# A fused attention and expert kernel: gate logits of three units worked on in their PSUM bank, and the last listed tile behind all dense tiles

## The chip, the cores and the metric

The kernel runs on one core of a Trainium2 chip. The metric is the time of one execution on the device, in microseconds; lower is better. A core has TensorE (PE: matmuls; PEld its weight loads), VectorE (DVE), ScalarE (ACT), GpSimd (POOL) and SyncE (SP, which here only starts transfers). Each works through its own queue in order; semaphores tie them together.

## What is computed

Four batches of 11,456 rows of 128 numbers go through two steps of attention by way of 49 agents, and each resulting row then through one of eight experts, the one with the largest gate logit:

```python
def _attn_ref(q, k, v, agents):
    def sm(a, b):
        s = scale * (a @ b.transpose(0, 2, 1))
        s = s - s.max(-1, keepdims=True)
        e = np.exp(s)
        return e / (e.sum(-1, keepdims=True) + 1e-09)
    return sm(q, agents) @ (sm(agents, k) @ v)

# x: the 45,824 rows of the attention; F = 1024
logits = x @ w_gate                                  # 8 experts
expert_idx = np.argmax(logits, axis=1)
probs = softmax(logits)                              # + 1e-09 in the sum
y[row] = probs[row, e] * (np.maximum(x[row] @ w1[e], 0) @ w2[e])   # e = expert_idx[row]
```

## The kernel before

**Tiles and stages.** A batch is 90 blocks of 128 rows. Ten blocks are a *unit* (`UB`), nine units a batch. For each batch come: the agents' scores against the keys (`k_ops`), the agents' sums over the values (`v_ops`), the queries' scores and exponentials (`q_head`, one unit at a time, stored to memory and read back transposed as `et`), the gates, the routing (`r_ops`: which expert each row has, and lists), and the experts.

**Dense and listed tiles.** In each batch most rows have the same expert. Every row is first put through it: `dense_tile` takes 4, 4 and 2 blocks of a unit (`MACROS`), stores the result and so fills the whole output. The rows whose expert is another are listed; a *listed* tile (`min_tile`) of 128 of them is gathered, put through its expert, and scattered over the dense result by POOL (L1430). `CAP` allows 8, 5, 1 and 1 listed tiles for the four batches. A loop over the batches (`seq`, `ready`) sets the order of dense and listed tiles: the tiles of batches 0 to 2 are mixed into the next batch's dense tiles, that of batch 3 goes in after `(3, 8, 0)`, the first 4 blocks of its last unit.

**An expert tile.** Layer one goes into an `hp` bank pair (L1194 and, for the small terms, L1203; L1187 to L1189 in a listed tile). ACT makes the rounded half `hhi` (L1223), DVE the remainder `hlo` (L1228), which frees `hp`. Layer two adds both in `yp` (L1211, L1212, L1217), of which there is one buffer; ACT copies it to `yo` (L1328), POOL multiplies by the gate `isc` (L1333), SP stores (L1338, L1341).

**The gates.** `q_tail` does a unit: ten matmuls (L925) give, for each row, eight high parts of the logits, eight low parts and a sum, 17 numbers in the PSUM bank `misc`; ACT copies the high parts to `lg` in SBUF (L930), DVE adds the low parts (L933) and puts the sum into `sm` (L934). Then the bank is free. `gate_ops` does two units (`GP = 2`) from SBUF: the largest logit (L950), the reciprocal (L951), the difference (L952), the product (L953), the exponential on ACT (L956), and the gate `isc` (L960 to L964), all on DVE.

**One bank for many.** PSUM has one `misc` buffer. Scores (L372 to L374), agent sums (L514), gates, routing counts (L1141) and the turned rows of listed tiles (L1405) all pass through it, one at a time.

**The order of the work.** The functions only record operations, with a cost, a key (when it is due) and the buffers they take and use. `Plan.run` then lays them out for all engines at once: of the operations that are ready and no more than `WINDOW = 20` keys ahead, it takes the one that can start first by those costs, and an operation that takes a buffer waits until the last user of the old one is done (`RINGS` says how many buffers there are). So a change of one cost or one buffer can change the order everywhere.

Of the kernel before, what the change touches and what calls it, by code (L numbers as in the profile page):

```python
# [56 lines left out]
GP = 2  # L57
# [147 lines left out]
def agent_attention_moe(ctx: ExitStack, tc: tile.TileContext, qT, kT, v, agT, wg, w1, w2, out):  # L205
# [620 lines left out]
    def q_begin(t, key):  # L826
        t.glg, t.gsm, t.gisc = Gen("lg"), Gen("sm"), Gen("isc")

        def begin():
            t.lg = buf("lg", [P, NBLK, NE])  # L830
            t.sm = buf("sm", [P, NBLK])
# [5 lines left out]
        t.o_qb = PL.op("POOL", 1.0, begin, key, new=[t.glg, t.gsm, t.gisc])  # L837
# [79 lines left out]
    def q_tail(t, u, k):  # L917
        U = t.U[u]
        r = Rec()
        gp = Gen("misc")  # L920

        def lo():
            p = r.l = misc([P, UB, LW])
            for j in range(UB):
                nc.tensor.matmul(p[:, j], U.et.bitcast(F16)[0:A2, j * P:(j + 1) * P], t.G, start=True, stop=True)  # L925

        sl = slice(u * UB, (u + 1) * UB)

        def lc():
            nc.scalar.copy(t.lg[:, sl], r.l[:, :, 0:NE])  # L930

        def la():
            nc.vector.tensor_tensor(t.lg[:, sl], r.l[:, :, NE:2 * NE], t.lg[:, sl], op=OP.add)  # L933
            nc.vector.tensor_scalar(t.sm[:, sl], r.l[:, :, 2 * NE], 1e-9, None, op0=OP.add)  # L934
        U.o_lo = o = PL.op("PE", 0.26, lo, k, U.o_et + [t.o_G, t.o_qb], new=[gp], use=[U.gt, t.gG])
        o = PL.op("ACT", act(UB * NE), lc, k, [o, t.o_qb], use=[gp, t.glg])
        U.o_lg = PL.op("DVE", 0.36, la, k, [o], use=[gp, t.glg, t.gsm])


    def gate_ops(t, u0, u1, k):  # L940
# [3 lines left out]
        g3, g4 = Gen("gz"), Gen("gr")  # L944

        def g1():
            z = r.z = buf("gz", [P, GP * UB, NE])[:, 0:n]
            rs = r.rs = buf("gr", [P, 3, GP * UB])[:, :, 0:n]
            lg = t.lg[:, sl]
            nc.vector.tensor_reduce(rs[:, 2], lg, axis=AX.X, op=OP.max)  # L950
            nc.vector.reciprocal(rs[:, 0], t.sm[:, sl])  # L951
# [3 lines left out]
        def g2():  # L955
            nc.scalar.activation(r.z, r.z, AF.Exp, scale=1.0 / SW)  # L956
# [13 lines left out]
        for U in t.U[u0:u1]:  # L970
            U.o_gate = o
# [699 lines left out]
```

## Time and profile before

| | |
|---|---|
| three runs | 1016.14, 1010.60, 1016.64 us; median 1016.14 |
| the profiled execution | 1012.58 us, its span 1010.7 us |
| PE busy | 940.8 us, 93% of the span |
| DVE, ACT, POOL busy | 733.0, 661.6, 515.1 us |
| granted PE clock, mean | 0.98 |

The profile is of one execution. Busy time of PE counts matmuls whose ends are modelled, so where PE is busy it need not run at its best. A row of the time line gives start, duration, engine, line, operation, output and input, count, and in brackets the idle time of that engine just before with what ended it. In a row by line, busy time and the mean in ns of one stand behind the first bar, the idle time before it and its releasers behind the second. A row of waits gives the total, the number of times and the longest. Where an engine waits for several, the last to come is named.

### The profile page before, as it was taken

How to read it: one execution, taken by the hardware profiler on the slowest of the kernel's cores; microseconds unless marked ns; L12 is line 12 of the kernel's file. 1: busy time of each engine (PE TensorE's matmuls, PEld its weight loads, DVE VectorE, ACT ScalarE, POOL GpSimd, SP SyncE). 2: the span in 40 equal slices, each digit the busy share in tenths (PEclk: the TensorE clock that was granted, in tenths of full speed). 3: DMA queues.
4: the chain of work that ended last, by engine and by line, in shares of the span. 5: the costliest groups of instructions: out<-in, count | busy, mean ns of one | idle time of the engine just before them, and what ended most of it. 6: DMA issues, size and time to landing. Idle time of an engine off the chain costs nothing. (4 is left out here: it accounts for less than half of the span.)

```text
span 1010.7 us, 34717 instructions
## 1 busy us (share of the span) xinstructions
PE 940.8 (93%) x14953; PEld 766.1 (76%) x14953; DVE 733.0 (73%) x1148; ACT 661.6 (65%) x898; POOL 515.1 (51%) x721
## 2 busy tenths in 40 slices
PE   5789998999899999999998998999999999999895
PEld 4668876877678877878777887888877788777674
DVE  7656677588996677566899767676788966778852
ACT  6457986877686777644576777764666667656453
POOL 4124988555495988332345488742234535321321
PEclk9999998999999999999999999999999999999998
DMA  9636788885579566565444926881444635331211
GB/s 339 203 116 228 237 276 226 249 256 197 177 236 251 168 196 192 146 184 174 112 134 128 311 76 185 208 233 39 133 115 108 175 91 143 77 93 45 71 28 31
DMA packets 157261, 166.41 MB, mean 165 GB/s; under 512 B 60618, under 2 KB 130503, under 8 KB 157098
## 3 DMA queue, kind: packets, MB, share of 16 engines
q1 hardware_dynamic: 155658, 163.17, 54.0%
q8 instruction: 119, 1.95, 0.8%
q0 software_dynamic: 1440, 0.93, 0.5%
q14 instruction: 44, 0.36, 0.1%
HBM read 99.73 MB, written 45.57 MB: 144 GB/s over the span
## 5 line engine op out<-in xcount | busy, mean ns | idle before, releaser
L1228 DVE SCALAR_TENSOR_TENSOR hlo<-hp,hhi 128x1024 f16<-128x1024 f32 x375 | 445.9, 1218 | 180.9 <-ACT hhi L1223 178.5
L1223 ACT ACTIVATE hhi<-hp 128x1024 f16<-128x1024 f32 x375 | 368.9, 1023 | 161.5 <-PE hp L1203 142.8
L1211 PE MATMUL yp<-Wd,hhi 128*128 128x128 f16 x2880 | 354.3, 222 | 1.2 <-ACT yo L1328 0.7
L1212 PE MATMUL yp<-Wd,hhi 128*128 128x128 f16 x2880 | 352.9, 222 | 0.0
L1211 PEld LDWEIGHTS <-hhi 128*128 128x128 f16 x3000 | 293.7, 99 | 32.8 <-issue 29.7
L1212 PEld LDWEIGHTS <-hhi 128*128 128x128 f16 x3000 | 298.0, 99 | 2.5 <-issue 2.1
L1333 POOL TENSOR_TENSOR yo<-yo,isc 128x256 f32<-128x256 f32 x180 | 112.6, 643 | 235.6 <-ACT yo L1328 183.9
L1194 PE MATMUL hp<-et,Md 128*128 128x512 f16 (+1 forms) x864 | 195.0, 346 | 22.9 <-DVE hlo L1228 22.7
L352 POOL TENSOR_TENSOR clo<-cf,chi 128x512 f16<-128x512 f32 x186 | 185.1, 1026 | 54.2 <-ACT chi L344 43.9
L1217 PE MATMUL yp<-Wd,hlo 128*128 128x128 f16 x2880 | 192.9, 219 | 0.5 <-DVE hlo L1228 0.5
L1217 PEld LDWEIGHTS <-hlo 128*128 128x128 f16 x3000 | 176.2, 98 | 2.8 <-issue 1.5
L1194 PEld LDWEIGHTS <-Md 128*128 128x128 f16 x864 | 75.0, 98 | 63.7 <-issue 30.2
L1328 ACT COPY yo<-yp 128x512 f32<-128x512 f32 (+1 forms) x108 | 55.7, 516 | 71.1 <-PE yp L1217 54.3
L876 POOL TENSOR_TENSOR rows<-xs,rows 128x245 f16<-128x245 f32 x72 | 46.8, 670 | 99.6 <-ACT rows L871 93.7
L344 ACT CAST chi<-cf 128x1280 f16<-128x1280 f32 x62 | 78.3, 1264 | 6.9 <-DMA cf<-in_qT 4.6
L1203 PE MATMUL hp<-etq,Mq 19*128 19x512 f16 (+1 forms) x864 | 72.1, 352 | 0.0
L1203 PEld LDWEIGHTS <-Mq 19*128 19x128 f16 x864 | 18.8, 91 | 69.6 <-issue 69.6
L374 PEld LDWEIGHTS <-clo 128*128 128x128 f16 x670 | 54.2, 97 | 3.3 <-POOL clo L352 3.0
L372 PE MATMUL misc<-a,chi 128*128 128x49 f16 x630 | 55.7, 184 | 0.6 <-DVE xt L1426 0.5
L374 PE MATMUL misc<-a,clo 128*128 128x49 f16 x630 | 55.5, 184 | 0.7 <-POOL clo L352 0.7
L373 PE MATMUL misc<-a,chi 128*128 128x49 f16 x630 | 55.4, 185 | 0.0
L372 PEld LDWEIGHTS <-chi 128*128 128x128 f16 x630 | 50.4, 96 | 5.0 <-issue 3.2
(263 smaller groups left out, 1167.2 us busy)
## 6 DMA issues: line engine op xcount, KB each, us to landing
cf<-in_kT SPq DMA_DIRECT2D x36, 640.0 KB
cf<-in_v SPq DMA_DIRECT2D x35, 640.0 KB
cf<-in_qT SPq DMA_DIRECT2D x35, 640.0 KB
out<-yo SPq DMA_DIRECT2D x72, 256.0 KB
eb<-rows SPq DMA_DIRECT2D x36, 320.0 KB
wf<-in_w SPq DMA_DIRECT2D x16, 512.0 KB
vst<-parts SPq DMA_DIRECT2D x15, 512.0 KB
wst<-parts SPq DMA_DIRECT2D x15, 512.0 KB
```

The costliest lines, as they stand in the source:

```text
L344: nc.scalar.copy(st.hi[:, i * n:(i + 1) * n], f)
L352: (nc.gpsimd if pool else nc.vector).tensor_tensor(st.lo[:, o], f[:, d], st.hi[:, o], op=OP.subtract)
L372: nc.tensor.matmul(p[:, j], h, t.a[:, 0], start=True, stop=False)
L374: nc.tensor.matmul(p[:, j], l, t.a[:, 0], start=False, stop=True)
L1194: nc.tensor.matmul(hp[:, c:c + n], m[:, fb * P:(fb + 1) * P], e, start=c % 512 == 0, stop=False)
L1203: nc.tensor.matmul(hp[:, c:c + n], m[r:r + R2, fb * P:(fb + 1) * P], e[r:r + R2], start=False, stop=(c + n) % 512 == 0)
L1211: nc.tensor.matmul(y, h, w[:, fb * 256 + P:(fb + 1) * 256], start=first and j == 0 and i == 0, stop=False)
L1212: nc.tensor.matmul(y, h, w[:, fb * 256:fb * 256 + P], start=False, stop=False)
L1217: nc.tensor.matmul(yp[:, j * P:(j + 1) * P], lo[:, c + j * P:c + (j + 1) * P], w[:, fb * 256:fb * 256 + P], start=False, stop=last and j = ...
L1223: nc.scalar.activation(hi, hp, AF.Relu)
L1228: nc.vector.scalar_tensor_tensor(lo, hp, 0.0, hi, op0=OP.max, op1=OP.subtract)
L1333: nc.gpsimd.tensor_tensor(v3[:, j:j + 2], v3[:, j:j + 2], t.isc[:, k0 + j:k0 + j + 2, 1:2].bitcast(F32).to_broadcast([P, 2, P]), op=OP.mult)
```

## The change

`q_tail` goes. `gate_ops` does what it did and more, for the units in `GROUPS`: unit 0, units 1 and 2, units 3 to 5, units 6 to 8. Up to 30 blocks' logits (510 numbers a row) lie in one `misc` bank. ACT copies the high parts to a new tile `lm`; DVE adds them to the low parts in the bank, adds 1e-9 to the sums in the bank, and takes reciprocal, largest logit, difference and product from there; only the product is written to SBUF, in `lg`. The bank is free after that sixth instruction. The exponential reads `lg` and writes `gz`. The last step, `isc`, moves from DVE (one instruction) to POOL (two). Routing reads `lg`, which now holds the product in place of the difference; it tests for zero in both cases.

Batch 3's listed tile is called for at `(3, 8, 8)`, the last blocks of its last unit, and is no longer held back by `gap`. The scatter (L1428 in the changed kernel) depends on all stores recorded before it, so now on all of batch 3's. Three smaller edits: `an` and `idx` have one buffer, and a listed tile takes its `xt` buffer with the matmul before it and not with ACT's copy.

```diff
-GP = 2
+GP = 3
-RINGS = {... "an": 2, ... "lg": 2, "sm": 2, "idx": 2, ...}
+RINGS = {... "an": 1, ... "lg": 2, "idx": 1, ...}
...
-    def q_tail(t, u, k):
...
     def gate_ops(t, u0, u1, k):
...
+        def lo():
+            p = r.l = misc([P, GP * UB, LW])[:, 0:n]
+            for i, U in enumerate(us):
+                for j in range(UB):
+                    nc.tensor.matmul(p[:, i * UB + j], U.et.bitcast(F16)[0:A2, j * P:(j + 1) * P], t.G, start=True, stop=True)
+
+        def lc():
+            r.m = buf("lm", [P, GP * UB, NE])[:, 0:n]
+            nc.scalar.copy(r.m, r.l[:, :, 0:NE])
 
         def g1():
...
-            lg = t.lg[:, sl]
-            nc.vector.tensor_reduce(rs[:, 2], lg, axis=AX.X, op=OP.max)
-            nc.vector.reciprocal(rs[:, 0], t.sm[:, sl])
-            nc.vector.tensor_tensor(lg, lg, rs[:, 2, :, None].to_broadcast([P, n, NE]), op=OP.subtract)
-            nc.vector.tensor_tensor(z, lg, rs[:, 0, :, None].to_broadcast([P, n, NE]), op=OP.mult)
+            l = r.l[:, :, NE:2 * NE]
+            nc.vector.tensor_tensor(l, l, r.m, op=OP.add)
+            nc.vector.tensor_scalar(r.l[:, :, 2 * NE], r.l[:, :, 2 * NE], 1e-9, None, op0=OP.add)
+            nc.vector.reciprocal(rs[:, 0], r.l[:, :, 2 * NE])
+            nc.vector.tensor_reduce(rs[:, 2], l, axis=AX.X, op=OP.max)
+            nc.vector.tensor_tensor(l, l, rs[:, 2, :, None].to_broadcast([P, n, NE]), op=OP.subtract)
+            nc.vector.tensor_tensor(t.lg[:, sl], l, rs[:, 0, :, None].to_broadcast([P, n, NE]), op=OP.mult)
...
+        def g5():
+            rs = r.rs
             sv = t.isc[:, sl, 1:2].rearrange("p k o -> p (k o)").bitcast(F32)
-            nc.vector.scalar_tensor_tensor(sv, rs[:, 0], t.isig, rs[:, 1], op0=OP.mult, op1=OP.mult)
+            nc.gpsimd.tensor_tensor(rs[:, 0], rs[:, 0], rs[:, 1], op=OP.mult)
+            nc.gpsimd.tensor_scalar(sv, rs[:, 0], t.isig, None, op0=OP.mult)
...
-            o = PL.op("PE", 0.12, mm, k + 1, [o, t.o_av2], new=[gx], use=[gec, t.gav2])
-            o = PL.op("ACT", act(P), hi, k + 1, [o], new=[x.gxt], use=[gx])
+            o = PL.op("PE", 0.12, mm, k + 1, [o, t.o_av2], new=[gx, x.gxt], use=[gec, t.gav2])
+            o = PL.op("ACT", act(P), hi, k + 1, [o], use=[gx, x.gxt])
...
-    ready = {(1, 2, 0): 0, (2, 2, 0): 1, (3, 2, 0): 2, (3, 8, 0): 3}
+    ready = {(1, 2, 0): 0, (2, 2, 0): 1, (3, 2, 0): 2, (3, 8, 8): 3}
...
-                if wait and gap >= 6:
+                if wait and (gap >= 6 or c == B - 1):
...
+    GROUPS = ((0, 1), (1, 3), (3, 6), (6, 9))
...
-                q_tail(t, u, k + 6)
-            if u % GP == 1 or u == NU - 1:
-                gate_ops(t, u - u % GP, u + 1, k + 8)
+            for u0, u1 in GROUPS:
+                if u == u1 - 1 and (t.b or u > 2):
+                    gate_ops(t, u0, u1, k + 7)
```

What the planner makes of it shows in the queues. First DVE at the start of the program, where the gates of batch 0's unit 0 meet the first expert tiles; before:

```order
L1228 SCALAR_TENSOR_TENSOR hlo<-hp,hhi 128x1024
L933 TENSOR_TENSOR lg<-misc,lg 128x80
L934 TENSOR_SCALAR sm<-misc 128x10
L1228 SCALAR_TENSOR_TENSOR hlo<-hp,hhi 128x1024
L859 TENSOR_REDUCE qm<-misc 128x10
L863 TENSOR_TENSOR xs<-misc,qm 128x490
```

and now (line numbers are those of the changed kernel; `lm` is the copy of the high parts, `gr` holds maxima and reciprocals):

```order
L1226 SCALAR_TENSOR_TENSOR hlo<-hp,hhi 128x1024
L937 TENSOR_TENSOR misc<-misc,lm 128x10x8
L938 TENSOR_SCALAR misc<-misc 128x10
L939 RECIPROCAL gr<-misc 128x10
L940 TENSOR_REDUCE gr<-misc 128x10
L941 TENSOR_TENSOR misc<-misc,gr 128x10x8
L942 TENSOR_TENSOR lg<-misc,gr 128x80
L1226 SCALAR_TENSOR_TENSOR hlo<-hp,hhi 128x1024
```

Six instructions on the bank stand between the two `hlo` where two stood. Second, DVE in batch 1, the gates of units 4 and 5 before, and of units 3 to 5 now (`vacc` are the agent sums of batch 2, which use the same bank); before:

```order
L1228 SCALAR_TENSOR_TENSOR hlo<-hp,hhi 128x1024
L933 TENSOR_TENSOR lg<-misc,lg 128x80
L934 TENSOR_SCALAR sm<-misc 128x10
L950 TENSOR_REDUCE gr<-lg 128x20
L951 RECIPROCAL gr<-sm 128x20
L952 TENSOR_TENSOR lg<-lg,gr 128x160
L953 TENSOR_TENSOR gz<-lg,gr 128x160
L960 TENSOR_REDUCE gr<-gz 128x20
L961 TENSOR_SCALAR gr<-gr 128x20
L962 RECIPROCAL gr<-gr 128x20
L964 SCALAR_TENSOR_TENSOR isc<-gr,isig 128x20
L524 TENSOR_TENSOR vacc<-vacc,misc 49x129 x2
```

and now:

```order
L1226 SCALAR_TENSOR_TENSOR hlo<-hp,hhi 128x1024
L937 TENSOR_TENSOR misc<-misc,lm 128x30x8
L938 TENSOR_SCALAR misc<-misc 128x30
L939 RECIPROCAL gr<-misc 128x30
L940 TENSOR_REDUCE gr<-misc 128x30
L941 TENSOR_TENSOR misc<-misc,gr 128x30x8
L942 TENSOR_TENSOR lg<-misc,gr 128x240
L949 TENSOR_REDUCE gr<-gz 128x30
L950 TENSOR_SCALAR gr<-gr 128x30
L951 RECIPROCAL gr<-gr 128x30
L1226 SCALAR_TENSOR_TENSOR hlo<-hp,hhi 128x1024
L524 TENSOR_TENSOR vacc<-vacc,misc 49x129 x2
```

The bank is free after the second of the gate's rows before, after the sixth now; on PE's queue the agent sums' matmuls follow the 30 gate matmuls behind 16 matmuls of layer two and 8 of layer one. Third, POOL at the end of the program (`yo` multiplies, then the scatter of batch 3's listed tile); before:

```order
L1333 TENSOR_TENSOR yo<-yo,isc 128x256 x3
L1429 MEMSET spacer 1x1
L1430 DMA out<-yo,rt 45824x128
L1333 TENSOR_TENSOR yo<-yo,isc 128x256 x3
L1603 TENSOR_LOAD ovf
```

and now:

```order
L1331 TENSOR_TENSOR yo<-yo,isc 128x256 x6
L1427 MEMSET spacer 1x1
L1428 DMA out<-yo,rt 45824x128
L1601 TENSOR_LOAD ovf
```

The scatter stands behind the last dense multiply, and with it behind the last store, where three multiplies followed it.

More of the change, by code (lines that the diff above doesn't have):

```diff
@@ L61 @@
 BS = NU * US
-RINGS = {"misc": 1, "hp": 3, "yp": 1, "cf": 7, "chi": 2, "clo": 2, "xs": 2, "wf": 2, "vst": 2, "wst": 2, "an": 2, "av2": 4, "et": 5, "etq": 3,
+RINGS = {"misc": 1, "hp": 3, "yp": 1, "cf": 7, "chi": 2, "clo": 2, "xs": 2, "wf": 2, "vst": 2, "wst": 2, "an": 1, "av2": 4, "et": 5, "etq": 3,
          "rows": 2, "rt": 2, "ls": 2, "ix": 2, "er": 2, "ec": 2, "xt": 3, "hhi": 4, "hlo": 4, "yo": 4, "a16": 2, "af": 2, "qm": 2, "mh": 2,
-         "isc": 2, "G": 2, "lg": 2, "sm": 2, "idx": 2, "isig": 2, "bm": 2, "Md": 2, "Mq": 2, "Ml": 2, "Wd": 2, "ohx": 1, "oa": 2}
+         "isc": 2, "G": 2, "lg": 2, "idx": 1, "isig": 2, "bm": 2, "Md": 2, "Mq": 2, "Ml": 2, "Wd": 2, "ohx": 1, "oa": 2}
 class Op:
@@ L826, in q_begin @@
     def q_begin(t, key):
-        t.glg, t.gsm, t.gisc = Gen("lg"), Gen("sm"), Gen("isc")
+        t.glg, t.gisc = Gen("lg"), Gen("isc")
         def begin():
             t.lg = buf("lg", [P, NBLK, NE])
-            t.sm = buf("sm", [P, NBLK])
             t.isc = buf("isc", [P, NBLK, 4], I32)
@@ L836, in begin @@
             nc.gpsimd.memset(t.isc[:, :, 3:], 0)
-        t.o_qb = PL.op("POOL", 1.0, begin, key, new=[t.glg, t.gsm, t.gisc])
+        t.o_qb = PL.op("POOL", 1.0, begin, key, new=[t.glg, t.gisc])
         t.o_lg, t.o_gate, t.o_eb = [], [], []
@@ L914, in q_head @@
         U.o_et = [PL.op("ACT", act(UC), cp, k, [o], new=[gt], use=[gh])]
-    def q_tail(t, u, k):
[L918 to L937, printed above, removed]
     def gate_ops(t, u0, u1, k):
@@ L962, in g3_ @@
             nc.vector.reciprocal(rs[:, 1], rs[:, 1])
+        def g5():
+            rs = r.rs
             sv = t.isc[:, sl, 1:2].rearrange("p k o -> p (k o)").bitcast(F32)
-            nc.vector.scalar_tensor_tensor(sv, rs[:, 0], t.isig, rs[:, 1], op0=OP.mult, op1=OP.mult)
+            nc.gpsimd.tensor_tensor(rs[:, 0], rs[:, 0], rs[:, 1], op=OP.mult)
+            nc.gpsimd.tensor_scalar(sv, rs[:, 0], t.isig, None, op0=OP.mult)
         c = n * NE * 0.00107
-        o = PL.op("DVE", 0.7 + 3 * c, g1, k, [U.o_lg for U in t.U[u0:u1]], new=[g3, g4], use=[t.glg, t.gsm])
+        o = PL.op("PE", 0.04 + 0.3 * (u1 - u0), lo, k, [o for U in us for o in U.o_et] + [t.o_G, t.o_qb], new=[gp], use=[U.gt for U in us] + [t.gG])
+        for U in us:
+            U.o_lo = o
+        o = PL.op("ACT", act(n * NE), lc, k, [o, t.o_qb], new=[gm], use=[gp])
+        o = PL.op("DVE", 0.62 + 4 * c, g1, k, [o], new=[g3, g4], use=[gm, gp, t.glg])
         t.o_lg.append(o)
-        o = PL.op("ACT", act(n * NE), g2, k, [o], use=[g3])
-        o = PL.op("DVE", 0.85 + c, g3_, k, [o, t.o_sig], use=[g3, g4, t.gsig, t.gisc])
-        for U in t.U[u0:u1]:
+        o = PL.op("ACT", act(n * NE), g2, k, [o], use=[g3, t.glg])
+        o = PL.op("DVE", 0.4 + c, g3_, k, [o], use=[g3, g4])
+        o = PL.op("POOL", 0.35, g5, k, [o, t.o_sig], use=[g4, t.gsig, t.gisc])
+        for U in us:
             U.o_gate = o
@@ L1550, in agent_attention_moe @@
     t0.U[1].ld[0].after.append(t0.o_vl[-1])
-    q_tail(t0, 1, -934)
     q_head(t0, 2, -936, True)
```

11 lines of the change are left out of this document (6 added, 5 removed).

## The prediction

> **What bounds the kernel now.** I read the page first, for the busy shares of the engines.
>
> ```profile
> span 1010.7 us, 34717 instructions
> PE 940.8 (93%) x14953; PEld 766.1 (76%) x14953; DVE 733.0 (73%) x1148; ACT 661.6 (65%) x898; POOL 515.1 (51%) x721
> ```
>
> TensorE (PE) is busy for 940.8 of 1010.7 us, and the change leaves its matmuls as they are. So the change can only move the 70 us in which PE stands. Next come the waits of PE, and a table of stretches, which says where they are.
>
> ```profile
> PE hp L1194 <- DVE hlo L1228: 22.7, 22, 3.6
> PE misc L514 <- DVE xs L863: 5.1, 2, 4.2
> 0.00:25.00 25.00, 12.93 (x270) 11.72 (x270) 18.34 (x43) 16.48 (x19) 11.41 (x24) 1.00 0.93 341
> 250.00:300.00 50.00, 45.99 (x691) 35.52 (x689) 47.30 (x68) 37.56 (x46) 33.27 (x36) 0.97 0.66 215
> 700.00:750.00 50.00, 50.00 (x725) 39.32 (x722) 37.90 (x75) 29.21 (x42) 10.95 (x17) 1.00 0.38 109
> 1000.00:1011.00 11.00, 0.32 (x6) 0.14 (x3) 0.00 (x0) 0.37 (x1) 0.62 (x1) 0.68 0.12 32
> ```
>
> In a row of stretches the busy times follow as PE, PEld, DVE, ACT, POOL. The first 25 us (12 lost) and the last 11 (10.7 lost) are the load and the drain. In between PE loses 4 us in 250 to 300, where VectorE (DVE) is busy for 47.3 of 50, and nothing in 700 to 750. The stalls are local: mostly layer one of the experts (L1194) waiting for DVE's `hlo`, which frees the `hp` bank, and some waits for the one `misc` bank.
>
> The largest single wait of the middle is at 172 us, and the time line of DVE, POOL, ACT and PE around it shows what makes it.
>
> ```profile
> 164.20 5.07 DVE L952 TENSOR_TENSOR lg<-lg,gr 128x160 f32<-128x160 f32 x1
> 165.34 3.75 POOL L501 TENSOR_TENSOR S<-S,m 128x245 f32<-128x245 f32 x6
> 169.66 0.34 ACT L956 ACTIVATE gz<-gz 128x160 f32<-128x160 f32 x1 [4.25 <-DVE gz L953]
> 172.06 1.32 PE L514 MATMUL misc<-cf,S 128*49 128x129 f32 x10 [4.16 <-DVE xs L863]
> ```
>
> L952, the gates' subtraction, both of whose operands are in SBUF, stood from 164.20 to 169.27, until POOL's row of tensor operations ended at 169.1. ACT's exponential stood behind it for 4.25 us and PE for 4.16. The spread of each line says whether this is the rule.
>
> ```profile
> L952 DVE TENSOR_TENSOR lg<-lg,gr x20: 236/261/5070, 83.2 to 918.2; 128x160 f32<-128x160 f32 x16, 128x80 f32<-128x80 f32 x4
> L953 DVE TENSOR_TENSOR gz<-lg,gr x20: 241/326/3002, 83.5 to 918.4; 128x160 f32<-128x160 f32 x16, 128x80 f32<-128x80 f32 x4
> L933 DVE TENSOR_TENSOR lg<-misc,lg x36: 219/231/242, 63.8 to 917.6; 128x80 f32<-128x80 f32 x36
> ```
>
> The columns are least, median and longest ns. L933, of the same kind but with one operand in PSUM, never took over 242 ns in 36 times; L952 and L953 went up to 5070 and 3002. In this trace, only the two with both operands in SBUF stand behind POOL.
>
> The Trainium skill's page SBUF — State Buffer, section SBUF: two separate sides, says that a DVE instruction with two SBUF inputs and a GpSimd instruction that reads SBUF take turns on one port pair, each for its whole instruction. By it alone a wait would end with the POOL instruction under way; the 5.07 us outlasted a whole row of them, so the trace has more at stake than the page, and I go by the trace.
>
> **The change part by part.** *The locked pair goes.* L941 and L942 of the changed kernel do the same arithmetic with one operand in PSUM, as L933 does. Besides the 5.07 us, the long cases of L952 and L953 (3.00 at most) stand ahead of PE's waits at 370 to 372, 619 and 801 us:
>
> ```profile
> 370.00 0.28 PE L1217 MATMUL yp<-Wd,hlo 128*128 128x128 f16 x2 [0.49 <-DVE hlo L1228]
> 372.47 0.23 PE L1405 MATMUL misc<-ident,er 128*98 128x128 f16 x1 [0.51 <-DVE xs L863]
> 618.96 0.18 PE L372 MATMUL misc<-a,chi 128*128 128x49 f16 x1 [0.54 <-DVE xt L1426]
> 801.64 0.39 PE L1194 MATMUL hp<-et,Md 128*128 128x512 f16 x1 [1.48 <-DVE hlo L1228]
> 613.94 0.23 PE L1405 MATMUL misc<-ident,er 128*98 128x128 f16 x1 [2.34 <-ACT yo L1328]
> ```
>
> 4.16 + 0.49 + 0.51 + 0.54 + 1.48 = 7.2 us gained. Bounds: 4.2 (the first alone) and 7.2.
>
> *A wait with no cover.* The last row quoted is a transpose into `misc` right behind ten gate matmuls that had just filled it. In the new order no gate group is followed at once by another user of `misc`; the wait of 2.3 us goes.
>
> *Fewer instructions on DVE.* The rows by line, with their sums (three rows of ACT end the list):
>
> ```profile
> L952 DVE TENSOR_TENSOR lg<-lg,gr 128x160 f32<-128x160 f32 (+1 forms) x20 | 14.2, 712 | 0.0
> L953 DVE TENSOR_TENSOR gz<-lg,gr 128x160 f32<-128x160 f32 (+1 forms) x20 | 12.3, 615 | 0.7
> L933 DVE TENSOR_TENSOR lg<-misc,lg 128x80 f32<-128x80 f32 x36 | 8.3, 232 | 3.7 <-ACT lg L930 3.7
> L934 DVE TENSOR_SCALAR sm<-misc 128x10 f32<-128x10 f32 x36 | 5.7, 157 | 0.0
> L950 DVE TENSOR_REDUCE gr<-lg 128x20 f32<-128x160 f32 (+1 forms) x20 | 6.0, 302 | 0.0
> L951 DVE RECIPROCAL gr<-sm 128x20 f32<-128x20 f32 (+1 forms) x20 | 5.1, 256 | 0.0
> L863 DVE TENSOR_TENSOR xs<-misc,qm 128x490 f32<-128x490 f32 x36 | 24.1, 668 | 2.8
> L930 ACT COPY lg<-misc 128x80 f32<-128x80 f32 x36 | 8.1, 226 | 6.9 <-PE misc L925 6.6
> L433 ACT COPY S<-misc 128x490 f32<-128x490 f32 x27 | 15.3, 568 | 4.7 <-PE misc L374 4.4
> L1223 ACT ACTIVATE hhi<-hp 128x1024 f16<-128x1024 f32 x375 | 368.9, 1023 | 161.5 <-PE hp L1203 142.8 <-PE hp L1189 16.9 <-ACT big L1031 0.8
> ```
>
> The first six rows sum to 51.6 us. In their place come 16 groups of six. Between L933 (80 elements, 232 ns) and L863 (490, 668) lies 1.06 ns an element, so a tensor operation on 240 takes 0.40 us. A group of three units costs three of these, a reduction of 0.40 (L950 with the same step), a scalar operation of 0.18 (L934) and a reciprocal of 0.28 (L951): 2.06; a group of one about 1.3, of two 1.7. Four batches: 4 x (1.3 + 1.7 + 2 x 2.06) = 28 us. So DVE sheds 23 us, 15 of them the stalls of L952 and L953 over their medians. Beyond the waits already counted this is worth something only where DVE is full (the row 250 to 300). Gate work stands there for a few us at most, so I take 1 us gained, between nothing and 6.
>
> An operation of DVE that writes PSUM has no row here. From below, it costs what one that reads PSUM does; L934, which reads it, is the shortest of the six rows with 157 ns. From above, twice L934's time, 0.16 us on three of the six in 16 groups: 7.5 us of DVE time, under the 23 shed. I take the lower.
>
> The Trainium skill speaks against this part: its page Perfetto Trace Analysis, section Optimizing Scalar/DVE Operations, puts DVE's fixed cost near 125 ns on PSUM and 60 on SBUF. Worked out from the page, an estimate, five operations moved to PSUM in 16 groups would add 5 us to DVE; the sum would be 1 us worse at most. L934's 157 ns leave little room for such a surcharge.
>
> *The start.* In DVE's queue, six instructions of unit 0's gates now stand ahead of an `hlo` where L933 and L934 stood; the rest of its gate work came only later.
>
> ```profile
> 63.82 0.23 DVE L933 TENSOR_TENSOR lg<-misc,lg 128x80 f32<-128x80 f32 x1
> 64.04 1.22 DVE L1228 SCALAR_TENSOR_TENSOR hlo<-hp,hhi 128x1024 f16<-128x1024 f32 x1
> 64.81 0.20 PE L372 MATMUL misc<-a,chi 128*128 128x49 f16 x1
> ```
>
> DVE starts the `hlo` some 0.9 us later, and the scores at 64.81 find the bank free 0.2 us later than they ask. I take 0.5 lost, from 0 to 1.3.
>
> *The bank is held longer.* With one `misc` bank, the next user on PE's queue waits for the arithmetic's end. A group of three holds it for ACT's copy (226 ns for 80 elements and 568 for 490 give 0.36 for 240) and 2.06 on DVE: some 2.5 us. If an activation of 1.02 us (L1223) and an `hlo` of 1.22 stand ahead on the two queues, 4.8. What covers it is the layer work that PE has queued between, at these rates:
>
> ```profile
> 991.71 1.06 PE L1217 MATMUL yp<-Wd,hlo 128*128 128x128 f16 x16
> 985.34 1.03 PE L1194 MATMUL hp<-et,Md 128*128 128x512 f16 x4
> 986.30 0.40 PE L1203 MATMUL hp<-etq,Mq 19*128 19x512 f16 x4
> ```
>
> In the new order the eight groups of three have between 2.3 us (16, 4 and 4 of just these, batch 1, units 3 to 5) and over 19 ahead of the next user; four have under 3.7: 2.3, 3.2, 3.5 and 3.6. Without queueing they lose 0.2 in all; with both queues ahead 2.5 + 1.6 + 1.3 + 1.2 = 6.6. I take half, 3.3 lost. ACT has 24 instructions fewer, at 65% busy I cost that at nothing.
>
> *The end.* Batch 3's listed tile now ends the program. The tile's 24 matmuls of layer one fill what was PE's wait for the last `yo` copy; its 24 of layer two come after the last dense tile.
>
> ```profile
> 990.59 1.05 POOL L1430 DMA_INDIRECT out<-yo,rt  x1 [3.12 <-DMA out<-yo]
> 1000.40 0.37 ACT L1328 COPY yo<-yp 128x256 f32<-128x256 f32 x1 [2.97 <-PE yp L1217]
> 1000.85 0.62 POOL L1333 TENSOR_TENSOR yo<-yo,isc 128x256 f32<-128x256 f32 x1 [2.13 <-ACT yo L1328]
> 1001.88 0.92 SPq L1341 DMA_DIRECT2D out<-yo  x1
> ```
>
> Its 48 matmuls are some 3 us at 1.06 for 16, so the last dense tile ends about 2.5 us earlier. But the scatter waits for the last dense store to land (3.1 us, as at 990.59) and takes 1.05 where the program ended with the store: 0 net, from 1 gained to 3 lost.
>
> *POOL.* The product with `isig` becomes 32 short instructions there, each of 30 elements at most, so under the 0.62 us of a 256-element `yo` multiply (just above). They stand ahead of the `yo` multiplies, which waited for the gate before too. POOL is 49% idle and four `yo` buffers cover it: nothing, at most 2 us.
>
> *Waits of the new order.* It is drawn up anew everywhere, and POOL still stands against DVE's two-operand instructions in the routing. A quarter of the 7.2 comes back elsewhere: 1.7 lost, from 0 to 5.
>
> Sum: -7.2 - 2.3 - 1 + 3.3 + 0.5 + 0 + 1.7 = -5.0 us. The profiled execution took 1012.58, so 1007.6. The three runs' median is 1016.14, and those three with the profiled one average 1014.0, from which the sum gives 1009.0. I put the time at 1008.5.
>
> **The rivals.** *A: DVE's relief reaches the full stretches.* The 23 us shed shorten the queue ahead of `hlo` wherever routing and gates meet. For it: 22.7 us of PE's waits are for `hlo`. Against: the routing's own instructions fill those stretches and stay. With 6 us gained there, and 0 to 5 lost to bank and new order: 1012.58 - 7.2 - 2.3 - 6 + 0.5 = 997.6, up to 1003.
>
> *B, slower: the bank becomes the bound.* Three units' logits sit in the one `misc` bank, and PE's queue, which is in order, stops at its next user: scores, agent sums or routing counts. All eight groups of three would lose 2.5 to 3.5 us (20 to 28), less 9.5 gained: 1023 to 1031. It decides from where hold exceeds cover, 3.6 us for half the groups. For it: the 2.34 us at 613.94 is this wait. Against: one such wait in 36 groups before.
>
> *C: nothing comes of it.* PE is 93% busy, and the waits struck out return one place further on, as with 700 to 750, where PE is full whatever DVE does: 1012 to 1014.
>
> **How the numbers follow.** The forecast has 0.49, A 0.24, B 0.15, C 0.12. About 1% is what a measurement here can tell from no change. Faster by more: A and the forecast's lower edge, 0.24 + 0.09 = 0.33. Slower by more: most of B, 0.13. The rest, 0.54, is within. The range takes in the forecast with its bounds, C, and all of A but its edge, and leaves out most of B: 998 to 1021.
>
> **What would show it.** Right: no tensor operation of the gates above 0.5 us; PE's waits behind `xs` and `xt` gone; DVE some 20 us less busy; PE's waits for `misc` behind gate groups under 4 us in all; an end some 12 us after the last dense tile's `yo` copy starts, not 10.3 (from 1000.40 to 1010.7). Wrong: gate operations that still stand behind POOL, or several waits of over 1 us by PE for L942.

## The result: slower by 1.2%

The kernel before took 1013.82 us (median of four, 1010.6 to 1016.64), the changed one 1026.75 (median of four, 1022.4 to 1031.04). The ratio is 1.012, with a 95% interval from 1.0083 to 1.0156. The forecast was 1008.5, with a range of 998 to 1021: the sign was wrong, and the time lies outside the range.

The profiled execution of the changed kernel took 1022.79 us and has a span of 1021.0 us, 10.3 more than before. First its page, then the waits of TensorE (PE): us in total, times, longest.

```profile
span 1021.0 us, 34667 instructions
PE 940.5 (92%) x14953; PEld 764.0 (75%) x14953; DVE 715.5 (70%) x1060; ACT 658.2 (64%) x874; POOL 528.1 (52%) x753
```

```profile
PE hp L1192 <- DVE hlo L1226: 31.1, 29, 3.6
PE misc L454 <- DVE m L448: 3.0, 2, 2.5
PE misc L514 <- POOL S L501: 2.8, 1, 2.8
PE yp L1209 <- ACT yo L1507: 2.3, 1, 2.3
PE misc L372 <- DVE mx L438: 1.9, 2, 1.7
...
PE misc L514 <- DVE lg L942: 0.8, 1, 0.8
...
PE misc L372 <- DVE lg L942: 0.5, 1, 0.5
```

PE is as busy as before (940.5 against 940.8 us) and VectorE (DVE) has 17.5 us less to do, yet PE waits more. The view's rows sum to 66.0 us, where before had 58.6 (+7.4). The last copy to `yo` begins at 1007.99, where PE's work ends, and 13.0 us of drain follow it; before, 10.3 us followed it (from 1000.40). These +2.7 and the +7.4 make up all but 0.2 of the difference. By tile, the waits for `misc` fell from 20.3 to 14.6 us, those for `yp` rose from 1.5 to 6.6, and those for `hlo`, which is L1192 here and was L1194, from 22.7 to 31.1. The largest growth is in the `hlo` row.

What the change set out to remove is gone. The three tensor operations of the gates, by line (least, median, longest ns):

```profile
L937 DVE TENSOR_TENSOR misc<-misc,lm x16: 230/368/417, 62.6 to 925.8; 128x240 f32<-128x240 f32 x8, 128x80 f32<-128x80 f32 x4, 128x160 f32<-128x160 f32 x4
L941 DVE TENSOR_TENSOR misc<-misc,gr x16: 249/374/417, 63.5 to 927.2; 128x240 f32<-128x240 f32 x8, 128x80 f32<-128x80 f32 x4, 128x160 f32<-128x160 f32 x4
L942 DVE TENSOR_TENSOR lg<-misc,gr x16: 241/366/408, 63.8 to 927.6; 128x240 f32<-128x240 f32 x8, 128x80 f32<-128x80 f32 x4, 128x160 f32<-128x160 f32 x4
```

None exceeds 417 ns, where L952 went to 5070. But other instructions of DVE stand behind POOL, one of them nearly as long. The time line of DVE, POOL and PE around 135 us, and of DVE and PE around 590:

```profile
134.65 3.85 DVE L438 TENSOR_TENSOR mx<-mx,S 128x490 f32<-128x490 f32 x1
133.86 2.92 POOL L352 TENSOR_TENSOR clo<-cf,chi 128x512 f16<-128x512 f32 x3
136.73 1.24 POOL L875 TENSOR_TENSOR rows<-xs,rows 128x245 f16<-128x245 f32 x2
140.72 0.59 PE L1192 MATMUL hp<-et,Md 128*128 128x512 f16 x2 [3.61 <-DVE hlo L1226]
589.47 1.02 DVE L1446 TENSOR_SCALAR fx<-ls 128x5 f32<-128x5 f32 x1
590.52 1.07 DVE L1447 SCALAR_TENSOR_TENSOR fx<-ls,fx 128x5 f32<-128x5 f32 x1
592.86 0.18 PE L372 MATMUL misc<-a,chi 128*128 128x49 f16 x1 [1.71 <-DVE mx L438]
```

L438 is the last unit's running maximum, with both operands in SBUF; 3845 ns is its longest here. L1446 has five elements a partition and took at most 1020 ns against a median of 158. The trace before had such cases too; there the longest of L438 (1657 ns, at 142.27 us) and of L995 (1859 ns, at 218.13 us) stood beside rows of POOL:

```profile
L438 DVE TENSOR_TENSOR mx<-mx,S x4: 669/813/1657, 25.9 to 631.4; 128x490 f32<-128x490 f32 x4
L995 DVE SCALAR_TENSOR_TENSOR big<-lg,em x4: 901/902/1859, 218.1 to 918.6; 128x720 f32<-128x720 f32 x4
218.07 2.94 POOL L1380 TENSOR_TENSOR vst<-wf,vst 128x512 f16<-128x512 f32 x2
```

Taken over all of DVE outside the gates, the time above the least duration of each form (counted where it is over 0.1 us) is 22.7 us before and 23.0 after. So DVE does not stand longer outside the gates as a whole; it stands at other places. The program came out in another order, and in it the stall at 172 us is replaced by one at 141.

A second place shows what a larger group can do. At a batch's end the routing waits for the last gates; the old grouping leaves unit 8 alone there, the new one puts units 6 to 8. DVE of the kernel before, and then of the changed one, happen to reach this place at the same time:

```profile
498.98 0.23 DVE L933 TENSOR_TENSOR lg<-misc,lg 128x80 f32<-128x80 f32 x1
499.95 0.90 DVE L995 SCALAR_TENSOR_TENSOR big<-lg,em 128x720 f32<-128x720 f32 x1
502.60 2.35 DVE L1228 SCALAR_TENSOR_TENSOR hlo<-hp,hhi 128x1024 f16<-128x1024 f32 x2
503.87 0.59 PE L1194 MATMUL hp<-et,Md 128*128 128x512 f16 x2 [0.36 <-DVE hlo L1228]
```

```profile
498.99 0.41 DVE L937 TENSOR_TENSOR misc<-misc,lm 128x240 f32<-128x240 f32 x1
501.19 0.91 DVE L993 SCALAR_TENSOR_TENSOR big<-lg,em 128x720 f32<-128x720 f32 x1
503.68 2.34 DVE L1226 SCALAR_TENSOR_TENSOR hlo<-hp,hhi 128x1024 f16<-128x1024 f32 x2
504.94 0.59 PE L1192 MATMUL hp<-et,Md 128*128 128x512 f16 x2 [0.93 <-DVE hlo L1226]
```

From the first gate instruction to the next `hlo` are 3.62 us before and 4.69 after, and PE waits 0.93 instead of 0.36.

### The profile page after: what moved, and what is told of

The parts are those of the page before. It is cut to its first block, busy times and chain, and to the rows that moved or that the text cites. A ratio compares the mean times of both kernels' runs of the same rounds, so it can differ in the third digit from the quotient of the medians.

```text
span 1021.0 us, 34667 instructions
## 1 busy us (share of the span) xinstructions
PE 940.5 (92%) x14953; PEld 764.0 (75%) x14953; DVE 715.5 (70%) x1060; ACT 658.2 (64%) x874; POOL 528.1 (52%) x753
## 5 line engine op out<-in xcount | busy, mean ns | idle before, releaser
L1192 PE MATMUL hp<-et,Md 128*128 128x512 f16 (+1 forms) x864 | 195.7, 345 | 31.4 <-DVE hlo L1226 31.1
L352 POOL TENSOR_TENSOR clo<-cf,chi 128x512 f16<-128x512 f32 x186 | 188.5, 1043 | 60.3 <-ACT chi L344 56.3
L1192 PEld LDWEIGHTS <-Md 128*128 128x128 f16 x864 | 75.1, 98 | 70.9 <-issue 41.8
```

Of the source, the lines that this page charges most:

```text
L352: (nc.gpsimd if pool else nc.vector).tensor_tensor(st.lo[:, o], f[:, d], st.hi[:, o], op=OP.subtract)
L1192: nc.tensor.matmul(hp[:, c:c + n], m[:, fb * P:(fb + 1) * P], e, start=c % 512 == 0, stop=False)
```

## The experiments

The question was which of the change's parts costs the time: the end, POOL's part, the arithmetic, or the order that came with it. Ratios are to the kernel before, run beside each on the same chip; the 95% interval stands in brackets.

### The two parts apart, and two pieces of the gates in the unchanged order

The first kernel is the old one with the new end:

```diff
-    ready = {(1, 2, 0): 0, (2, 2, 0): 1, (3, 2, 0): 2, (3, 8, 0): 3}
+    ready = {(1, 2, 0): 0, (2, 2, 0): 1, (3, 2, 0): 2, (3, 8, 8): 3}
-                if wait and gap >= 6:
+                if wait and (gap >= 6 or c == B - 1):
```

> The kernel before with only the last part of the change: batch 3's listed tile goes behind all of its dense tiles. Everything ahead of the last two dense tiles is ordered as before. Theory 'end' (the end costs what the traces show: 15.0 us instead of 10.3 after the last dense tile's yo copy, less the 2.5 to 2.8 us by which that tile ends earlier): 2 us slower than the kernel before, 1 to 4. Rival (the loss of the change sits at the end altogether): 8 to 13 us slower. As the prediction had it (0, from 1 gained to 3 lost): within 3 us.

The second undoes just these lines in the changed kernel.

> The changed kernel with the listed tile back in its old place; the gates' part of the change is whole, and the order ahead of the last two dense tiles is that of the changed kernel. Theory 'the middle' (most of the loss is PE's longer waits for hlo, 31.1 us against 22.7): 8 to 11 us slower than the kernel before, 2 us faster than the changed kernel. Rival 'end': no slower than the kernel before.

Measured: the new end alone 1.0006 [0.9977, 1.0034]; the changed kernel without it 1.0092 [1.0068, 1.0116]. The end costs some 3 us at most by its interval, and the gates' part is most of the loss.

The third puts both operands back in SBUF, in exactly the changed kernel's order:

```diff
-            l = r.l[:, :, NE:2 * NE]
-            nc.vector.tensor_tensor(l, l, r.m, op=OP.add)
+            l = t.lg[:, sl]
+            nc.vector.tensor_tensor(l, r.l[:, :, NE:2 * NE], r.m, op=OP.add)
```

> The changed kernel in exactly its own order on all five engines, but the sum of the logits is written to SBUF (lg), so that the reduction and the subtraction read SBUF again, and the subtraction and the product have both operands in SBUF as before. Theory 'what the change removes was worth something, the new order took more' : 4 to 10 us slower than the changed kernel, since the two instructions stand behind POOL again. Rival 'the stalls were never on the path': within 3 us of the changed kernel. Rival 'bank' (the arithmetic in the bank holds up PE): faster by 2 to 6 us, since the bank is free after four of the six instructions... the reciprocal and the addition of 1e-9 are the last that touch it.

Measured: 1.0136 [1.0112, 1.0161], against 1.012 for the changed kernel. The subtraction and the product do stand behind POOL again, but not long:

```profile
L941 DVE TENSOR_TENSOR lg<-lg,gr x16: 243/408/942, 64.6 to 930.1; 128x240 f32<-128x240 f32 x8, 128x80 f32<-128x80 f32 x4, 128x160 f32<-128x160 f32 x4
L942 DVE TENSOR_TENSOR lg<-lg,gr x16: 243/407/1161, 64.8 to 930.5; 128x240 f32<-128x240 f32 x8, 128x80 f32<-128x80 f32 x4, 128x160 f32<-128x160 f32 x4
```

The longest are 0.94 and 1.16 us, not 5.07 and 3.00. In the new order the lock between these two and POOL is worth too little to tell, so the 5 us stall came from where they stood in the old order as much as from their operands. The loss stands with the old operands too, so the arithmetic in the bank is not the bulk of it; a part of 3 us either way would not show.

The fourth returns the product with `isig` to DVE (one instruction behind the reciprocal) and leaves POOL's place in the plan empty.

> The changed kernel in its own order, but the product with isig is one VectorE instruction behind the reciprocal, as in the kernel before, and the two POOL instructions are gone (16 more instructions on VectorE, 32 fewer on POOL). Theory 'POOL's queue' (POOL stands 45.6 us in 11 waits for gr at L956, and what is queued behind it comes late): 4 to 10 us faster than the changed kernel. Theory 'order' (the loss is how the new order lines up VectorE's long stretches with PE's demand): within 3 us of the changed kernel.

Measured: 1.0106 [1.0079, 1.0133], within 3 us of the changed kernel. POOL's queue is not the bulk of the loss, although POOL waits 45.6 us for `gr` in the changed kernel. It is not ruled out as a part: DVE is busy for 4.6 us more here (720.1 against 715.5), which by the rates measured below costs 3 to 5 us, and what POOL's part is worth may hide behind them.

### Other orders, and half the gates' work

Two kernels only reorder. The first has the old gates and just the two small edits; the second has the changed kernel's instructions with another key.

```diff
-                    gate_ops(t, u0, u1, k + 7)
+                    gate_ops(t, u0, u1, k + 8)
```

> The kernel before with only the two small edits: an and idx with one buffer each, and the xt buffer claimed by the matmul ahead of its copy instead of by the copy. The gates' arithmetic is untouched; but the plan comes out otherwise from the second batch on. Theory 'any new order moves the time by as much' : 3 to 12 us away from the kernel before, on either side, with PE's waits for hlo changed by several us. Rival 'three units in one group': within 3 us of the kernel before.

> The changed kernel with one number of the plan altered: the gates' key is k + 8 instead of k + 7. All instructions are the same, in another order. Theory 'any new order': 3 to 12 us away from the changed kernel, either way. Theory 'three units in one group': within 3 us of the changed kernel, since the groups are as long as ever.

Measured: the small edits alone 0.9939 [0.99, 0.9979]; the other key 1.012 [1.0086, 1.0153]. So a new order can move the time by 6 us with the same arithmetic, but both orders with groups of three are slower by the same 1.2%. They are not new from the start: PE's queue is that of the kernel before for the first 5663 of its 14,953 matmuls in the one, and that of the changed kernel for the first 4568 in the other.

```diff
-    GROUPS = ((0, 1), (1, 3), (3, 6), (6, 9))
+    GROUPS = ((0, 1), (1, 3), (3, 5), (5, 7), (7, 9))
```

> The changed kernel, its groups of units 3 to 8 cut into three groups of two instead of two of three; a new order follows. Theory 'three units in one group' (the long burst of gate arithmetic comes ahead of hlo in VectorE's queue, and the last group ahead of the routing): 6 to 10 us faster than the changed kernel. Theory 'any new order': anywhere from 1008 to 1028, with no tie to the length of a group's arithmetic.

Measured: 1.0064 [1.0029, 1.0099], half the loss. (A second order with groups of two, further down, costs nearly the whole loss.)

The next one leaves most of the gates' work out, without a change of order. Only the addition, the maximum and the difference stay on DVE; the difference goes straight to `lg`, and one fill with ones takes the place of POOL's two products. The main lines that go:

```diff
-            nc.vector.tensor_scalar(r.l[:, :, 2 * NE], r.l[:, :, 2 * NE], 1e-9, None, op0=OP.add)
-            nc.vector.reciprocal(rs[:, 0], r.l[:, :, 2 * NE])
...
-            nc.vector.tensor_tensor(t.lg[:, sl], l, rs[:, 0, :, None].to_broadcast([P, n, NE]), op=OP.mult)
...
-            nc.vector.tensor_reduce(rs[:, 1], r.z, axis=AX.X, op=OP.add)
```

> The changed kernel in its own order, with gate work left out: of VectorE's nine instructions for a group only the addition, the maximum and the subtraction stay (the reciprocals, the product with them and the gate's last sum are left out), and POOL's two are one fill with ones. So VectorE has some 14 us less to do in bursts of half the length. Theory 'three units in one group': 4 to 9 us faster than the changed kernel. Theory 'order' (the lines that make hlo late are those of the routing and the agents, in a new alignment): within 3 us of the changed kernel.

Measured: 0.9952 [0.9923, 0.998], some 17 us below the changed kernel, for 24.8 us less work on DVE. Its page and its `hlo` row:

```profile
PE 935.1 (93%) x14953; PEld 762.6 (76%) x14953; DVE 690.7 (69%) x964; ACT 658.1 (66%) x874; POOL 519.4 (52%) x737
PE hp L1192 <- DVE hlo L1226: 23.5, 21, 3.6
```

The `hlo` waits fall from 31.1 to 23.5 us. The order as such was my theory here, and it expected 3 us at most; it falls in that form, and the other theory's 4 to 9 us were too few. What the gates do is on PE's path. That it is their work on DVE, and not the product that POOL is spared here, has to come from kernels that add work to DVE alone.

### Is that so in the old order too?

Four kernels tell whether DVE's time counts more in the new order: work taken away and work added, each in its own kernel's order. The one without the second step leaves out the sum, its 1e-9 and the reciprocal, and the first of POOL's two products. The added work is the maximum taken three or four times:

```diff
-            nc.vector.tensor_reduce(rs[:, 2], l, axis=AX.X, op=OP.max)
+            [nc.vector.tensor_reduce(rs[:, 2], l, axis=AX.X, op=OP.max) for _ in range(4)]
```

> The kernel before in its own order, with the same gate work left out as in the changed kernel with half its gates: of VectorE's rows only the additions, the maximum and the subtraction stay (the additions of 1e-9, the reciprocals, the product, the gate's sum are left out), and isc is filled with ones by VectorE. By the rows of the kernel before that takes 40 us from VectorE (5.7 + 5.1 + 12.3 + 5.9 + 4.8 + 5.3, and part of 5.0). Theory 'new order stands closer' (in the old order the gates' work lies where VectorE has slack, in the new one ahead of hlo that PE wants at once): no more than 5 us faster than the kernel before, against about 15 for the changed kernel with half its gates. Rival 'VectorE's time counts everywhere' (any us taken from VectorE gives PE half a us, in either order): 12 to 20 us faster than the kernel before.

> The changed kernel in its own order; left out are the gates' second step on VectorE (sum, 1e-9, reciprocal: 14.2 us in 48 instructions) and the first of POOL's two products. All six instructions of the first step stay. If the burst of the first step is what counts (2 us in a row ahead of an hlo): within 3 us of the changed kernel. If VectorE's time counts wherever it stands: 14.2 of the 26.7 us left out in the changed kernel with half its gates, so 7 to 9 us faster than the changed kernel.

> The kernel before in its own order, with the maximum of each gate group taken three times instead of once: 40 more instructions of 302 ns, 12.1 us more on VectorE and nothing else. Theory 'new order stands closer': within 3 us of the kernel before. Rival 'VectorE's time counts everywhere': 5 to 8 us slower.

> The changed kernel in its own order, with the maximum of each gate group taken four times instead of once: 48 more instructions of 283 ns, 13.6 us more on VectorE, in the bank and ahead of what stands behind a group. Both theories: 6 to 10 us slower than the changed kernel; if neither holds (what the halved gates gained came from elsewhere, such as POOL no longer waiting for the gates), within 3 us.

| kernel | ratio to before | DVE busy against its base, us | time against its base, us | us per us |
|---|---|---|---|---|
| before, half the gates | 0.989 [0.9858, 0.9921] | -27.1 | -11 | 0.4 |
| before, work added | 1.0061 [1.0039, 1.0084] | +11.3 | +6 | 0.55 |
| changed, half the gates | 0.9952 [0.9923, 0.998] | -24.8 | -17 | 0.7 |
| changed, no second step | 1.0014 [0.9987, 1.004] | -13.5 | -11 | 0.8 |
| changed, work added | 1.028 [1.0239, 1.0322] | +15.8 | +16 | 1.0 |

The base is 1 for the kernel before and 1.012 for the changed one, 1% being 10.1 us; the busy times are the pages'. The rival "DVE's time counts everywhere" came nearer than its opposite: in the old order too, gate work costs about half a us a us. Its sizes were off all the same: the halved gates gave 11 us where it said 12 to 20, and in the changed kernel the second step gave 11 instead of 7 to 9 and the added work cost 16 instead of 6 to 10. In the new order a us costs more. The single rows do not show it, as their intervals overlap and the base of 1.012 has one of its own (0.0036, or 4 us, either way). From the halved gates to the added work, which needs no base, it is 33 us for 40.6 us of busy time in the changed kernel, or 0.8, and 17 for 38.4 in the kernel before, or 0.45; the intervals of these two, some 0.1 either way, do not meet.

What is counted as DVE's time in the new order is not `hlo` alone, for the added work also holds the bank, and the halved gates spare POOL its products too. PE's waits for it behind gate groups, 1.3 us in the changed kernel, become 9.1, about half of the 16 us:

```profile
PE misc L372 <- DVE lg L942: 4.0, 4, 1.8
PE misc L514 <- DVE lg L942: 4.0, 3, 2.1
PE misc L1139 <- DVE lg L942: 1.1, 1, 1.1
```

Holding the bank some 1 us longer in each group of three (three more reductions, each 0.35 us in the changed kernel and 0.41 here) is enough to bring up rival B's mechanism.

### One stall removed, and more orders

The stall at 134.65 can be removed cleanly: the running maximum reads the bank, as it does for the other units, and the masked rows are filled there.

```diff
-                    nc.vector.memset(t.S[TAIL:, NBLK - 1], NEG)
-                nc.vector.tensor_tensor(t.mx, t.S[:, 0:UB] if u == 1 else t.mx, t.S[:, sl] if u == NU - 1 else r.p, op=OP.max)
+                    nc.vector.memset(t.S[TAIL:, NBLK - 1], NEG); nc.vector.memset(r.p[TAIL:, UB - 1], NEG)
+                nc.vector.tensor_tensor(t.mx, t.S[:, 0:UB] if u == 1 else t.mx, r.p, op=OP.max)
```

> The changed kernel in its own order; only the last unit's running maximum of each batch (L438) reads its scores from the bank, as those of the other units do, instead of the copy S in SBUF (one short fill of the bank's masked rows more, four times). In the changed kernel the one at 134.65 us took 3.85 us behind POOL's row, where 0.66 is usual, and PE then waited 3.61 us for hlo at 140.7. Theory 'the lock has moved': that wait goes, 3 to 6 us faster than the changed kernel, counting the lower clock behind the wait. Rival 'the wait at 140 us is due anyway' (the rest of VectorE's queue there is as long): within 2 us of the changed kernel.

Measured: 1.0133 [1.0101, 1.0166]; no gain. Its time line shows why, first DVE and PE at the place, then both some 240 us later:

```profile
135.47 0.67 DVE L438 TENSOR_TENSOR mx<-mx,misc 128x490 f32<-128x490 f32 x1
138.38 0.59 PE L1192 MATMUL hp<-et,Md 128*128 128x512 f16 x2 [0.65 <-DVE hlo L1226]
377.66 1.22 DVE L1226 SCALAR_TENSOR_TENSOR hlo<-hp,hhi 128x1024 f16<-128x1024 f32 x1 [1.03 <-ACT hhi L1221]
379.27 0.67 DVE L438 TENSOR_TENSOR mx<-mx,misc 128x490 f32<-128x490 f32 x1
380.08 0.23 PE L1403 MATMUL misc<-ident,er 128*98 128x128 f16 x1 [1.85 <-DVE mx L438]
```

L438 takes 0.67 us instead of 3.85, and PE's wait is 0.65 instead of 3.61: the cause at that place is shown. By the `yo` copies this kernel is 3.4 us ahead of the changed one at the end of unit 3 of batch 0. But now the bank stays taken until DVE gets to L438; in the next batches that stands behind an `hlo`, PE's next transpose waits 1.85 us, and in batch 2 it is 6 us behind. A lock was exchanged for a hold.

Two more kernels are further orders.

> The changed kernel with groups of two as in the run above, and the gates' key at k + 8: a third order for groups of two or three in the bank. Theory 'length of a group': 1016 to 1022, like the other run with groups of two. Theory 'each order has its own time, whatever the groups': anywhere from 1008 to 1030.

> The kernel before with one number of its plan altered, the gates' key k + 9 instead of k + 8: the same instructions in another order. Theory 'each order has its own time': 3 to 12 us away from the kernel before, either way, as the small edits alone were 6 us faster. Rival: within 3 us of it.

Measured: groups of two with key k + 8, 1.0107 [1.0071, 1.0143]; the kernel before with key k + 9, 0.9979 [0.9955, 1.0002]. The first is 1029.3 us, against the 1016 to 1022 of the theory "length of a group", which so fails: two units in a group can cost as much as three. The second is within 3 us of the kernel before, so that not every order has a time of its own.

The last two give the bank up early, and the plan knows it: the addition, 1e-9 and the reciprocal are one step, and the rest another, on SBUF.

```diff
-        o = PL.op("DVE", 0.62 + 4 * c, g1, k, [o], new=[g3, g4], use=[gm, gp, t.glg])
+        o = PL.op("DVE", 0.42 + c, g1, k, [o], new=[g3, g4], use=[gm, gp, t.glg])
+        o = PL.op("DVE", 0.20 + 3 * c, g1b, k, [o], use=[g3, g4, t.glg])
```

> The changed kernel's groups of three, but the sum of the logits goes to SBUF and the plan is told so: the bank is given up after three of VectorE's six instructions (addition, 1e-9, reciprocal), and the maximum, the subtraction and the product are a step of their own on SBUF, as in the kernel before. The order is drawn up anew. Theory 'the hold' (an order laid out around a bank that is held for all six instructions is what costs): 5 to 12 us faster than the changed kernel, 1010 to 1018, though the subtraction and product can stand behind POOL again. Theory 'the group' (three units' gates in one step, wherever the operands are): within 4 us of the changed kernel.

> The same early release with groups of two units. Theory 'the hold': as fast as early release with three, 1010 to 1018. Theory 'the group': as the earlier runs with groups of two, 1018 to 1028.

Measured: 1.0131 [1.0102, 1.0161] with groups of three, 1.0097 [1.0063, 1.0131] with two. Laying the order out around a long hold isn't the cause either. All the orders side by side, with PE's waits summed from the rows of the view:

| gates | orders and ratios | `hlo` waits, us | `misc` waits, us |
|---|---|---|---|
| logits unit by unit (old) | before 1; key k + 9 0.9979; small edits 0.9939 | 22.7; 22.9; 22.8 | 20.3; 19.8; 24.9 |
| two units in one step | 1.0064; 1.0107; early release 1.0097 | 27.1; 23.2; 28.5 | 21.3; 26.1; 21.6 |
| three units in one step | changed 1.012; k + 8 1.012; early release 1.0131 | 31.1; 36.4; 34.5 | 14.6; 15.9; 13.9 |

Here the line between them is clear: each of six orders with several units' logits, copy and arithmetic in one step is slower, by 0.6 to 1.3%, and none of the three with logits unit by unit. The waits are those of one execution each, and that of the small edits took 1016.91 us where the median of its ten is 1008.03. With groups of three the waits for `hlo` grow by 8 to 14 us, while those for the bank shrink by 4 to 6. With groups of two it is not one row: the order at 1.0107 has 23.2 us for `hlo`, hardly more than before, and 26.1 for the bank.

### A version faster than both

The old grouping with the small edits was 0.6% faster than the kernel before. On top of it, DVE's additions of 1e-9 were taken off:

```diff
-            nc.vector.tensor_scalar(t.sm[:, sl], r.l[:, :, 2 * NE], 1e-9, None, op0=OP.add)
+            nc.scalar.activation(t.sm[:, sl], r.l[:, :, 2 * NE], AF.Copy, bias=1e-9)
...
-            nc.vector.tensor_scalar(rs[:, 1], rs[:, 1], 1e-9, None, op0=OP.add)
```

> A version meant to be faster than both: the kernel before with the two small edits (6 us faster than the kernel before), in that order, with less of the gates' work on VectorE: the addition of 1e-9 to the first sum goes to ACT (36 instructions of 157 ns, 5.7 us, off VectorE), and that to the second sum, which is at least 1 and does not change by 1e-9 in 32 bits, is left out (20 of 239 ns, 4.8 us). By the two slopes measured in the old order (0.28 us a us taken away, 0.5 a us added), 10.5 us off VectorE give 3 to 5 us: 1002 to 1006. If ACT's 36 more instructions stand in PE's way as much as VectorE's did: 1008.

Measured: 1010.23 us where the kernel before took 1016.02 on that chip, 0.9929 [0.9907, 0.9952]. It is faster than the kernel before by 0.7%, and so than the changed one by about 1.9% (through the kernel before; they did not run side by side), but not measurably faster than the small edits alone (0.9939). The slopes promised 3 to 5 us for the 10 taken off DVE; that step of mine failed, and 36 instructions more on ACT may have taken it, which no run separates.

## Why the prediction was wrong

**Step by step.** *The locked pair, 7.2 us:* the waits at 172, 370, 372, 619 and 802 us are gone in the form named. But the sentence under it, that only the two with both operands in SBUF stand behind POOL, was false in the trace it was read from: L438 and L995 did so there, with 1.66 and 1.86 us. In the new order L438 met a longer row, and the small steps of L1446 and L1447 stand as well. So does a step of the gates that the change left in SBUF: L950 took 1.03 us at 291.93 beside POOL's L1134, against a median of 0.18. That was one of my signs of being wrong. The page I cited, SBUF — State Buffer of the Trainium skill, lists under Who interferes with whom also copies and `tensor_scalar` in two-port modes, which I passed over; L1446, a `tensor_scalar` that took 1.02 us beside a row of three POOL instructions (L352, from 589.30), agrees with that, though no run here shows in which mode it ran.

*The wait without cover, 2.3:* gone, but a wait of 2.3 for a listed tile's `yo` copy (L1507, at 508.20) came.

*DVE's relief, 1 us for 23:* DVE's busy time fell by 17.5 us, near the 20 foretold, but 15 of that are the stalls, which are counted above. Short instructions of DVE overlap in the records (durations before sum to 781.2 us, the busy time is 733.0), so the gates' lines show more: 72.6 us before and 43.2 after, or 14 without the stalls. In the old order a us of busy time was worth 0.4 to 0.55, as rival A has it. The relief should then have been worth 1 us by the busy time and up to 8 by the lines, an estimate. If the term was mis-sized, it was towards too little gain, and it did not turn the sign. Working in PSUM cost next to nothing: 30 elements take L938 0.197 us there and L950 0.181 in SBUF.

*The bank, 3.3 lost:* 1.3 us of waits. Rival B's mechanism did not come about, but it is 1 us of hold away. *The start, 0.5 lost:* the first `yo` copy came 1.3 us earlier. *The end, 0:* 1.0006 agrees, to 3 us. But it ends 15.0 us after the start of the last dense tile's copy, not 12; POOL's queue waits until 1010.7 before the scatter, which fits the landing of the last stores. *POOL, nothing:* not contradicted by 1.0106, though a few us could hide there.

*Waits of the new order, 1.7 of 0 to 5:* this is the step that failed, and it carried the sign. The waits struck out above are 9.5 of the 58.6 us that the view before sums to, which leaves 49.1; the view after sums to 66.0. So 16.9 us of waits came with the new order, 1.3 of them for the bank behind gates and 2.3 for the listed tile's copy, which leaves 13.3 where I had put 1.7; `hlo` alone went from 22.7 to 31.1. With the relief that should have shortened them (1 to 8 us, the estimate above), the new order cost some 18 to 25. I had priced it as a quarter of what was removed, with no row behind the quarter.

**What is shown and what isn't.** Shown: neither the end, nor POOL's product, nor the operands' place, nor the length of the hold makes up the bulk of the loss; gate work costs time in either order, and more in the new one, where it holds the bank as well; and each of the six orders tried in which two or three units' gates are one step is slower. Shown at one place by taking it away is the stall of L438 beside POOL's row. Seen in the traces alone is that the last group, ahead of the routing, is three units long, 0.57 us of PE at the place compared. With half the gates on both sides the new order is still behind, 0.9952 to 0.989: some 6 us (2 to 11 by the intervals) belong to the order even without most of this work, although L952 still stands behind POOL in the old one, 5.12 us at its longest.

How the rest splits over places is open. So is whether the number of units in a step is the cause, or something else that the six orders share: the one step from logits to product, the tile `lm`, POOL's product in the plan. No run has the new steps unit by unit, and groups of two cost from half the loss to nearly all of it. Not tried either was a grouping in the bank that leaves unit 8 alone ahead of the routing.

## What to carry to other kernels

When an order is drawn up by a planner, an edit to a few instructions is an edit to the whole program; price the reordering from orders that differ by a key or a buffer alone (here from 0.6% faster to 0.4% slower) before believing a sum of a few stalls. A stall that two engines make by standing opposite each other belongs to the place, not to the instruction: removing it here, and again at 134 us, let others appear. And collecting short steps into one saves instructions, but can put a longer run ahead of whoever waits next.

## What the runs showed of the hardware

A stop of PE can cost more than its length. Around the 3.48 us wait that ends at 271.51 in the changed kernel, with PE's busy time first and the granted clock third from the end of each row:

```profile
268.00:270.00 2.00, 0.03 (x2) 0.00 (x0) 1.90 (x5) 1.65 (x2) 2.00 (x5) 1.00 0.40 146
272.00:274.00 2.00, 2.00 (x16) 1.12 (x15) 1.65 (x2) 0.90 (x1) 0.44 (x1) 0.50 0.41 159
274.00:276.00 2.00, 2.00 (x22) 2.00 (x20) 1.85 (x2) 1.98 (x3) 0.00 (x0) 0.50 0.29 115
276.00:278.00 2.00, 2.00 (x23) 2.00 (x22) 2.00 (x3) 0.00 (x0) 0.00 (x0) 0.56 0.03 8
278.00:280.00 2.00, 2.00 (x24) 1.11 (x22) 1.79 (x6) 1.87 (x3) 1.03 (x2) 1.00 0.00 0
```

PE works through the 6 us from 272 to 278 at 0.50 to 0.56 of its clock and so loses about 3 us more, an estimate from these rows. The 2.10 us wait that ends at 239.90 is followed by 4 us at 0.55 and 0.60:

```profile
240.00:242.00 2.00, 2.00 (x15) 1.30 (x14) 1.39 (x3) 1.55 (x4) 1.19 (x2) 0.55 0.93 355
242.00:244.00 2.00, 2.00 (x23) 1.85 (x22) 1.30 (x2) 0.96 (x3) 0.00 (x0) 0.60 0.48 139
```

The Trainium skill's page TensorE: Matmul & The Clock Gate, section What's actually happening, has the clock fall to half after an idle window of some 3.4 us. The first wait agrees; the second, of 2.1 us, was shorter than that and the clock fell all the same. Nor does the length of the wait decide alone: the clock stays at 1.00 around the 2.34 us wait that ends at 508.20.

```profile
508.20 0.22 PE L1209 MATMUL yp<-Wd,hhi 128*128 128x128 f16 x1 [2.34 <-ACT yo L1507]
506.00:508.00 2.00, 0.00 (x0) 0.00 (x0) 1.88 (x5) 2.00 (x3) 1.51 (x3) 1.00 0.94 223
508.00:510.00 2.00, 1.80 (x33) 1.80 (x33) 2.00 (x2) 0.15 (x1) 1.06 (x1) 1.00 0.95 321
```

The clock does not explain this result: it lost as much before (14.6 us of PE's busy time between 64 and 996 us, summed over windows of 2 us) as after (11.8).
